# A linear-attention layer with a feed-forward behind it on one core: w and u spread by products on two row halves, both chunks of a pair interleaved, six more transfers that transpose, and another order of all steps

## The chip, the cores and the metric

The kernel runs on one core of a Trainium2 chip. The metric is the device time of one execution in microseconds (us), the median of several runs; lower is better. The engines are TensorE (PE, matrix products and transposes; PEld is its weight load), VectorE (DVE), ScalarE (ACT), GpSimd (POOL) and SyncE (SP, which here only issues DMA transfers). Each engine works through its own list in order and waits by semaphores for the others.

## What is computed

Four batches of eight heads, 768 time steps, head size 48. First a recurrence per head, then a feed-forward over all 3072 tokens (384 features, 2048 hidden).

```python
for t in range(S):                                     # S = 768
    cur = einsum('bhd,bhe->bhde', u[None] * kt, vt)
    y[:, :, t] = einsum('bhd,bhde->bhe', rt, state + cur)
    state = w[None, :, :, None] * state + einsum('bhd,bhe->bhde', kt, vt)
x = y.transpose(0, 2, 1, 3).reshape(B * S, H * D)      # 3072 x 384
h = maximum(x @ w_in, 0.0)                             # 384 x 2048
out = h * h @ w_out                                    # 2048 x 384
```

All inputs and the output are float32 in memory; products run in bfloat16.

## The kernel before

**Units.** The time steps are cut into chunks of 128. A unit is one chunk of one batch, all eight heads: 24 units, listed in UNITS (line 17). Within a chunk the recurrence becomes products: with t the place in the chunk, r is scaled by w to the power t - 128 and k by w to the power 127 - t (factors Wt and Wk), so that the part within the chunk is a masked 128x128 product of r and k per head, times v, and the part of earlier chunks is r times a state S0W. The first four units (PAIRED) are two pairs, two chunks of one batch, loaded with rows of 384 bytes, of which partition p holds time steps 2p and 2p+1; there half of the partitions (64) belong to one chunk and half to the other.

**Steps of one unit** (methods of class Do, one name each): ld (line 319) loads r, k, v of one unit on SP's queue, lp (323) those of a pair. rh (339) and kh (336) scale r and k into a bfloat16 tile rk. P0 (342) is r times k, P1 (345) that times u, du (349) its sum per head, dv (352) v times du: the term of u. vb (357) is v in bfloat16. T (394) transposes rk by eight products with the identity and Tc (400) copies the result to rkT; XB (403) does the same as one DMA that transposes (crossbar transfer), on SP's queue. A (406) is the product of k and r per head, Bm (418) masks it out of PSUM. Y (421) sums the masked product times v, and for a batch's later chunks r times the state. xs (470) adds dv and writes bfloat16. X (486) transposes xs by three products and xTc (491) copies it to xT; xX (495) is one DMA that transposes instead. U (457) is k times v, and S0 (477), ts (480) and S (483) make the next state from it. For the pairs, TK and TR (360, 366) transpose k and r, KC and RC (369, 372) copy, Ap (375) and Bp (391) are A and Bm, and dv enters Y as a product with the identity (lines 427 to 432) instead of in xs.

**Feed-forward.** Units are gathered in groups of one or two (GROUPS). F1 (498) gives one bank of 512 hidden values by 12 products with 128 columns (group of one) or 6 with 256 (group of two), re (512) is the relu out of PSUM, sq (519) the square, F2 (526) four products with 384 columns that sum a quarter of the hidden values into the unit's output bank, os (574) copies it and out (577) stores it. The last unit's F2 is cut into column halves (Fh, COLS), with oh and outh. V and W (330, 333) load the two weight matrices on POOL's queue in four pieces each.

**Start.** w (256) loads the 384 values of w into one row, lw (265) takes their logarithm, bw (268) spreads the row to 128 partitions by a product with a row of ones in float32, and Wk and Wt (292, 296) are exponentials of that with a factor per partition. bc (300), WLcol (308) and WLm (311) make w to the power 128 in the shape of the state. u, bu and ub do the same for u. Z (563) are products without use that keep PE working. tab loads ACT's tables.

**Order.** ORDER (line 25) is a list written out by hand: each entry is step, engine (P, D, A, G for POOL, S) and buffer numbers. The loop at line 595 issues it as it stands, so each engine's list is the part of ORDER with its letter, and a step that waits holds back all that stand behind it on its engine, SP's transfers too.

```python
    for step in ORDER.split():
        what, how = step.split(":")
        name, *at = what.split(".")
        eng, *given = how.split("/")
```

## Time and profile before

| | |
|---|---|
| median of 3 runs | 170.84 us (170.64 to 170.85) |
| profiled execution | 171.19 us |
| its span, first to last instruction | 169.5 us |
| busy, of the span | PE 97%, DVE 81%, ACT 60%, POOL 59% |
| DMA queue of SP (q1) | 66.4% of 16 engines' span |
| weights' queue (q0) | 11.5% |
| granted TensorE clock | 1.0 |

Rows of the timeline read: start in us, duration in us, engine, line, operation, output<-inputs, shapes (partitions x elements), xcount, and in brackets the idle time before and what ended it. Rows by form end with busy us, mean ns of one, and the idle time of the engine before them. The digits under the page's slices are tenths of 40 equal parts of the span. A chain row is start, duration, engine and what it worked on. Times of matrix products in timeline rows overlap; the chain gives their spacing.

### The profile page before, as it was taken

Reading aid. Unit: us, or ns where it says so; the run is one execution under the profiler, and the core shown is the slowest. Engines: PE = TensorE matmul, PEld = TensorE weight load, DVE = VectorE, ACT = ScalarE, POOL = GpSimd, SP = SyncE. Lnnn points to the kernel's source line nnn. Section 1 sums busy time; section 2 is a strip of 40 time slices with the busy share of each in tenths; the row PEclk is TensorE's granted clock in tenths of the full one; section 3 lists DMA queues with packets and bytes.
Section 4 is the critical chain, followed back from the end, with each engine's and each line's share of the span. In section 5 each row is a group of like instructions: output and inputs, shape, how many; then the busy total and the mean of one; then the engine's idle time right before and its main releaser. Section 6 shows DMA issues by size and latency. Waiting matters only on the chain.

```text
span 169.5 us, 4602 instructions
## 1 busy us (share of the span) xinstructions
PE 164.2 (97%) x1828; PEld 125.4 (74%) x1828; DVE 137.1 (81%) x255; ACT 101.9 (60%) x190; POOL 99.9 (59%) x122
## 2 busy tenths in 40 slices
PE   4999999999999999999999999999999999999993
PEld 1686989767866786888766888766888676898762
DVE  5669989997899999979999999998779975955300
ACT  4684686870685779249892359952099393254731
POOL 6799681277199608996699979399627550200000
PEclk9999999999999999999999999999999999999999
DMA  5999999991899798999997999965959672230032
GB/s 136 323 237 193 215 215 208 201 200 39 165 200 211 138 191 173 209 201 134 209 203 151 212 228 220 177 136 141 184 98 202 170 88 70 90 99 0 6 139 93
DMA packets 96137, 27.56 MB, mean 163 GB/s; under 512 B 90642, under 2 KB 96020, under 8 KB 96116
## 3 DMA queue, kind: packets, MB, share of 16 engines
q1 hardware_dynamic: 92416, 22.55, 66.4%
q0 software_dynamic: 2816, 3.54, 11.5%
q10 hardware_dynamic: 884, 1.18, 2.2%
q8 instruction: 14, 0.23, 0.6%
q14 instruction: 7, 0.06, 0.1%
HBM read 20.45 MB, written 4.72 MB: 149 GB/s over the span
## 4 chain that ended last, share of the span: by engine, by line
PE 95%; ACT 1%; DVE 1%; issue 1%; ACTq 0%
PE bank L505 37%; PE bank L533 36%; PE bank L411 3%; PE bank L463 2%; PE bank L452 2%; PE bank L364 2%; PE bank L489 2%; PE bank L450 2%; PE bank L547 2%; PE bank L440 1%; PE bank L269 1%; DVE Bm L392 1%; PE bank L303 1%; PE bank L272 1%; PE bank L398 1%; PE bank L428 1%
## 5 line engine op out<-in xcount | busy, mean ns | idle before, releaser
L505 PE MATMUL bank<-xT,W 128*128 128x256 bf16 (+1 forms) x672 | 70.0, 257 | 0.0
L533 PE MATMUL bank<-W,hq 128*128 128x384 bf16 x368 | 68.9, 326 | 0.0
L505 PEld LDWEIGHTS <-W 128*128 128x128 bf16 x672 | 56.9, 98 | 7.7
L515 ACT ACTIVATE hr<-bank 128x512 bf16<-128x512 f32 x67 | 38.7, 594 | 36.4 <-PE bank L505 27.8
L533 PEld LDWEIGHTS <-hq 128*128 128x128 bf16 x368 | 33.8, 98 | 18.2
L522 ACT ACTIVATE hq<-hr 128x512 bf16<-128x512 bf16 x70 | 41.0, 626 | 3.4 <-DVE hr L517 2.8
L419 DVE TENSOR_TENSOR Bm<-bank,maskJT 128x512 bf16<-128x512 f32 x40 | 25.7, 682 | 2.7 <-PE bank L411 2.7
L355 POOL TENSOR_TENSOR dv<-ldv,du 128x384 f32<-128x384 f32 (+1 forms) x18 | 15.9, 891 | 16.2 <-DVE du L350 11.3
L517 DVE TENSOR_SCALAR hr<-bank 128x512 bf16<-128x512 f32 x29 | 19.7, 686 | 6.6 <-PE bank L505 4.5
L347 POOL TENSOR_TENSOR P<-P,ub 128x384 f32<-128x384 f32 x15 | 16.0, 1070 | 13.1 <-DVE P L343 12.7
L340 POOL TENSOR_TENSOR rk<-ldr,Wt 128x384 bf16<-128x384 f32 x15 | 16.4, 1101 | 0.0
L343 POOL TENSOR_TENSOR P<-ldr,ldk 128x384 f32<-128x384 f32 x13 | 13.3, 1023 | 1.5 <-DMA ldk<-in_k_dram 1.2
L524 DVE TENSOR_TENSOR hq<-hr 128x512 bf16<-128x512 bf16 x26 | 12.4, 490 | 2.0 <-ACT hr L515 1.8
L484 POOL TENSOR_TENSOR S0W<-ts,WLm 128x384 bf16<-128x384 f32 x10 | 10.9, 1091 | 4.4 <-DVE ts L481 3.6
L475 DVE TENSOR_TENSOR xs<-bank,dv 128x384 bf16<-128x384 f32 x20 | 11.1, 553 | 3.0 <-PE bank L452 1.1
L337 POOL TENSOR_TENSOR rk<-ldk,Wk 128x384 bf16<-128x384 f32 x12 | 12.3, 1032 | 1.4 <-DMA ldk<-in_k_dram 1.4
L350 DVE TENSOR_REDUCE du<-P 128x8 f32<-128x384 f32 x24 | 12.9, 542 | 0.0
L253 DVE COPY os<-bank 128x384 f32<-128x384 f32 x11 | 6.1, 551 | 6.9 <-PE bank L533 6.9
L481 DVE TENSOR_TENSOR ts<-bank,S0W 128x384 f32<-128x384 f32 x16 | 8.7, 550 | 1.2 <-POOL S0W L484 0.8
L452 PE MATMUL bank<-vb,Bm 128*128 128x48 bf16 x160 | 9.5, 183 | 0.0
L251 ACT COPY os<-bank 128x384 f32<-128x384 f32 (+2 forms) x14 | 6.3, 458 | 4.5 <-PE bank L533 2.5
L452 PEld LDWEIGHTS <-Bm 128*128 128x128 bf16 x160 | 8.2, 96 | 1.0
(79 smaller groups left out, 177.8 us busy)
## 6 DMA issues: line engine op xcount, KB each, us to landing
ldr<-in_r_dram SPq DMA_DIRECT2D x20, 192.0 KB, 4.0
ldk<-in_k_dram SPq DMA_DIRECT2D x20, 192.0 KB, 4.2
ldv<-in_v_dram SPq DMA_DIRECT2D x20, 192.0 KB, 3.6
out_dram<-os SPq DMA_DIRECT2D x12, 192.0 KB, 2.1
W<-in_moe_w_in_dram POOLq DMA_DIRECT2D x4, 384.0 KB, 8.6
W<-in_moe_w_out_dram POOLq DMA_DIRECT2D x4, 384.0 KB, 6.4
out_dram<-os ACTq DMA_DIRECT2D x5, 192.0 KB, 3.5
ldr<-in_r_dram SPq DMA_DIRECT2D x2, 384.0 KB, 4.1
```

Of the source, the lines that this page charges most:

```text
L340: e.tensor_mul(rk[slot[f"rk{i}"]][:, 0, :, 0:D], loaded("r", i), Do.factor("t", i % 2 if i < PAIRED else 2))
L343: e.tensor_mul(P0b[slot[f"P{i}"]], loaded("r", i), loaded("k", i))
L347: e.tensor_mul(t, t, bank("bu")[:, 0 : H * D].rearrange("p (h d) -> p h d", h=H) if i in EARLY_U else ub)
L350: e.tensor_reduce(dub[slot[f"dv{i}"]], P0b[slot[f"P{i}"]], axis=mybir.AxisListType.X, op=ALU.add)
L355: e.tensor_mul(dv_of(i) if i < PAIRED else dvb[slot[f"dv{i}"]], loaded("v", i), t)
L419: e.tensor_mul(Bmb[slot[f"Bm{i}{h}"]], heads(bank(f"bA{i}{h}"), 128), mask_b)
L452: e.matmul(y[:, hc, D * h : D * (h + 1)], m[h][:, hc, :], vb[:, 2 * hc + h, :], start=(c == 0), stop=True, skip_group_check=True,)
L505: e.matmul(hp[:, fi, :], W1[f // 4][:, c, 256 * (f // 2 % 2) : 256 * (f // 2 % 2 + 1)].rearrange("p (m j) -> p j m", j=2)[:, f % 2, :], xt ...
L515: e.activation(hr, hp, AF.Relu)
L517: e.tensor_scalar_max(hr, hp, 0.0)
L522: e.activation(hq, hr, AF.Square)
L533: e.matmul(bank(f"bO{i}")[:, 0:d_model], hqb[slot[f"hq{g},{f // m}"]][:, at : at + L], W2[q][:, f % 4, :], start=(seen[i] == 1 and f % 4 = ...
```

## The change

- **w and u.** Each is loaded as two rows of 192, on partition 0 and partition 64. bw and bu are two products each, one on each half of PE's rows, into two banks. The product now spreads the raw w, and the logarithm (lw) is taken afterwards, on 128 partitions, half by half; the exponentials read it from SBUF (LW) instead of from PSUM.
- **Pairs.** U of both chunks becomes UP, Y becomes YD (terms of dv and of the masked product, both chunks in turn, which use different row halves and different banks) and YI (the state's term, for the second chunk alone).
- **Transfers that transpose.** XB takes unit 9 as well (T.9 and Tc.9 go), xX the units 10 and 12 to 15 as well (X and xTc of these go).
- **Order.** All of ORDER is another one. Steps of one kind that move between engines, before and after: dv on DVE 6 and 12 of 24, kh 12 and 16, rh 9 and 12, P0 11 and 8, P1 9 and 8, vb 2 and 4; re on DVE 29 and 23 of 96, sq 26 and 34; os on DVE 11 and 7 of 23; outputs issued by ACT 6 and 12 of 23, by SP 15 and 11, by POOL 2 and none. T.5 stands on PE ahead of the first F1, where it stood behind fifteen feed-forward products. The first weights are issued on POOL behind WLm, P0.0 and P0.1. The last steps on PE are Fh with 288 columns, where they had 96. Memsets of the spare columns of rk and of WLm stand in the list, part of them behind rh.2.

```diff
-EARLY_U = ()
 ...
 ORDER = """
+mP.0:G nj:D w:A tab:A bw:P/0/1 u:A Z.4:P/2 lw.0:A Z.4:P/3 lp.r.1:S/1 lw.1:A Wt.0:A/4 lp.r.0:S/0 lp.k.0:S/0 rh.2:D/2
+Wk.0:A/5 lp.k.1:S/1 ld.k.5:S/4 Wk.1:A/6 mR:D mW:D mP.1:G mJ:G Wt.1:A/7 bc:P/0 WLcol:A WLm:G rh.0:D/0 P0.0:G/0 rh.1:D/1
+lp.v.0:S/0 kh.1:D/1 Wt.2:A bu:P/2/1 ub.0:A kh.0:D/0 rh.3:D/3 ub.1:A P1.0:D P0.3:D/1 du.0:D/0 P0.1:G/2 kh.3:D/3
+TR.0:P/3 RC.0:A/0 V.1:G TK.0:P/0 KC.0:A/1 TR.1:P/4 Ap.0.0:P/2/1 RC.1:A/2 P1.1:G kh.2:D/2 TK.1:P/7 V.0:G du.1:D/1
+Ap.0.1:P/3/0 Bp.0.0.0:D/0 vb.0:A/0 vb.1:A/1 KC.1:A/3 Bp.0.0.1:D/1 Bp.0.1.0:D/2 dv.1:G Bp.0.1.1:D/3 UP.0:P/6/5
+Ap.1.0:P/4/2 S0.0:D Ap.1.1:P/1/7 dv.0:G YD.0:P/3/0 V.2:G YI.1:P Wk.2:A P0.2:G/3 lp.v.1:S/1 vb.3:A/2 vb.2:A/3 xs.0:A/0
+Bp.1.0.1:D/4 Bp.1.0.0:D/5 kh.5:D/4 UP.1:P/6/2 X.0:P/3 xs.1:A/1 xTc.0:A/0 ld.r.5:S/4 rh.5:G/4 P1.3:D X.1:P/4 xTc.1:A/1
+T.5:P/0 Tc.5:A/4 F1.0.1:P/3 S0.2:D P1.2:G du.3:D/2 F1.1.1:P/4 F1.0.0:P/6 re.1.1:A/0 du.2:D/3 F1.1.0:P/0 Bp.1.1.0:D/6
+dv.3:G Bp.1.1.1:D/7 dv.2:G re.0.1:A/1 sq.0.1:D/0 re.1.0:A/2 YD.1:P/1/4 xs.2:A/2 A.5:P/7/3 ts.3:D/0 YI.3:P xs.3:A/3
+P0.5:D/4 F1.1.2:P/0 ld.r.4:S/5 V.3:G X.2:P/2 ts.1:D/1 xTc.2:A/0 ld.k.4:S/5 ld.k.8:S/6 X.3:P/1 sq.1.0:A/1 re.0.0:A/3
 ...
+X.6:P/7 F2.0.3:P/2 ld.v.9:S/0 os.0:A/3 XB.9:S/3 ld.r.11:S/3 rh.11:D/3 XB.8:S/0 vb.9:G/0 ld.k.11:S/3 xTc.6:D/2
+ld.r.14:S/7 Y.11:P/6 F2.6.3:P/0 F2.6.0:P/0 xs.10:D/0 vb.13:A/4 P1.11:G du.11:D/3 XB.12:S/1 dv.11:D xs.11:D/2 xX.10:S/1
 ...
+F2.21.1:P/1 sq.13.3:D/15 Fh.23.2.1:P/3 F2.18.2:P/7 os.21:A/1 out.21:S F2.22.2:P/6 Fh.23.3.1:P/3 F2.20.1:P/0
+F2.20.0:P/0 out.12:A out.19:A F2.22.0:P/6 oh.23.1:A/0 outh.23.1:A out.10:S os.20:D/2 out.20:A os.22:D/5 out.22:A
+Fh.23.1.0:P/5 Fh.23.3.0:P/5 Fh.23.2.0:P/5 Fh.23.0.0:P/5 oh.23.0:A/3 os.18:D/4 out.18:S outh.23.0:S
 """
-    Y=["bY{0}"], xs=["xs{0}"], U=["bU{0}"], ts=["ts{0}"], X=["bX{0}"], xTc=["xT"], xX=["xT"],
+    bw=["bW0", "bW1"], bu=["bu0", "bu1"], Y=["bY{0}"], xs=["xs{0}"], U=["bU{0}"], YD=["bY{x}", "bY{y}"], UP=["bU{x}", "bU{y}"], ts=["ts{0}"], X=["bX{0}"], xTc=["xT"], xX=["xT"],
-    bw=["bW"], Wk=["WkP{0}"], Wt=["WtP{0}"], bu=["bu"], bc=["bc"], Fh=["bO{0}{2}"], oh=["os{0}{1}"],
+    Wk=["WkP{0}"], Wt=["WtP{0}"], bc=["bc"], Fh=["bO{0}{2}"], oh=["os{0}{1}"],
 ...
-    wrow = const.tile([1, H * D], FP32, name="wrow")
-    lrow = const.tile([1, H, 64], FP32, name="lrow")
-    urow = const.tile([1, H * D], FP32, name="urow")
-    ones = const.tile([1, 128], FP32, name="ones")
+    wsrc = const.tile([128, H * D // 2], FP32, name="wsrc")
+    usrc = const.tile([128, H * D // 2], FP32, name="usrc")
+    LW = const.tile([128, H, DP], FP32, name="LW")
+    ones = const.tile([128, 128], FP32, name="ones")
     wcol = const.tile([128, HP], FP32, name="wcol")
     Wk = const.tile([128, H, D], FP32, name="Wk")
     Wt = const.tile([128, H, D], FP32, name="Wt")
     WLm = const.tile([128, HP, 2 * D], FP32, name="WLm")
 
-    nc.vector.memset(lrow[:, :, D:64], 0.0)
+    nc.vector.memset(LW[0:1, :, D:DP], 0.0)
     nc.vector.memset(ones, 1.0)
+    for t in rk[:PAIRED]:
+        nc.vector.memset(t[:, :, :, D:DP], 0.0)
 
     tcol_i = const.tile([128, 3], mybir.dt.int32, name="tcol_i")
     for c in range(2):
 ...
     nc.vector.tensor_copy(tcol, tcol_i)
     njcol = const.tile([128, 3], FP32, name="njcol")
-    nc.vector.tensor_scalar(njcol, tcol, -1.0, -1.0, op0=ALU.mult, op1=ALU.add)
     identity = const.tile([128, 128], BF16, name="identity")
     make_identity(nc, identity)
 ...
     mask_p = [per_pair(m) for m in maskP]
-    for t in rk:
-        nc.vector.memset(t[:, :, :, D:DP], 0.0)
-    nc.vector.memset(WLm, 0.0)
 
     E = {"A": nc.scalar, "D": nc.vector, "G": nc.gpsimd, "P": nc.tensor, "S": nc.sync}
 ...
+        def halves(e, t, row):
+            e.dma_start(
+                out=t.rearrange("(a q) n -> a q n", a=2)[:, 0, :],
+                in_=row.rearrange("h d -> (h d)").rearrange("(a n) -> a n", a=2),
+            )
+
         def w(e):
-            e.dma_start(out=wrow, in_=w.rearrange("h d -> (h d)").rearrange("(a n) -> a n", a=1))
+            Do.halves(e, wsrc, w)
 
         def u(e):
-            e.dma_start(out=urow, in_=u.rearrange("h d -> (h d)").rearrange("(a n) -> a n", a=1))
+            Do.halves(e, usrc, u)
+
+        def spread(e, t, to):
+            for h in range(2):
+                at = slice(64 * h, 64 * h + 1)
+                e.matmul(
+                    bank(f"{to}{h}")[:, 0 : H * D // 2], ones[at], t[at], start=True, stop=True, skip_group_check=True,
+                )
+
+        def bw(e):
+            Do.spread(e, wsrc, "bW")
+
+        def bu(e):
+            Do.spread(e, usrc, "bu")
+
+        def spread_half(to, h):
+            return bank(f"{to}{h}")[:, 0 : H * D // 2].rearrange("p (h d) -> p h d", d=D)
+
+        def ub(e, h):
+            copy(e, ub[:, HP * h : HP * (h + 1), :], Do.spread_half("bu", h))
 
         def tab(e):
             e.preload_act_table_set("natural_log_exp_and_others")
 
-        def lw(e):
-            e.activation(lrow[:, :, 0:D], wrow.rearrange("a (h d) -> a h d", h=H), AF.Ln)
-
-        def bw(e):
-            e.matmul(bank("bW")[:, 0 : H * D], ones, lrow[:, :, 0:D], start=True, stop=True)
-
-        def bu(e):
-            e.matmul(bank("bu")[:, 0 : H * D], ones, urow, start=True, stop=True)
-
-        def ub(e):
-            copy(e, ub.rearrange("p a b -> p (a b)"), bank("bu")[:, 0 : H * D])
+        def lw(e, h):
+            e.activation(LW[:, HP * h : HP * (h + 1), 0:D], Do.spread_half("bW", h), AF.Ln)
+
+        def nj(e):
+            e.tensor_scalar(njcol, tcol, -1.0, -1.0, op0=ALU.mult, op1=ALU.add)
+
+        def mR(e):
+            for t in rk[PAIRED:]:
+                e.memset(t[:, :, :, D:DP], 0.0)
+
+        def mW(e):
+            e.memset(WLm, 0.0)
 
 ...
+        def spreading(e, o, scale):
+            e.activation(o, LW[:, :, 0:D], AF.Exp, scale=scale)
+
         def Wk(e, n):
-            o = Do.factor("k", n).rearrange("p a b -> p (a b)")
-            e.activation(o, bank("bW")[:, 0 : H * D], AF.Exp, scale=njcol[:, n : n + 1])
+            Do.spreading(e, Do.factor("k", n), njcol[:, n : n + 1])
 
         def Wt(e, n):
-            o = Do.factor("t", n).rearrange("p a b -> p (a b)")
-            e.activation(o, bank("bW")[:, 0 : H * D], AF.Exp, scale=tcol[:, n : n + 1])
+            Do.spreading(e, Do.factor("t", n), tcol[:, n : n + 1])
 
         def bc(e):
 
             for hc in range(HP):
                 e.matmul(
-                    bank("bc")[:, hc : hc + 1], pair(lrow.rearrange("p (o a) b -> p o a b", o=1), 0, hc), ones[:, 0:1],
+                    bank("bc")[:, hc : hc + 1], pair(LW[0:1].rearrange("p (o a) b -> p o a b", o=1), 0, hc), ones[0:1, 0:1],
                     start=True, stop=True, skip_group_check=True,
                 )
 
 ...
-            e.tensor_mul(t, t, bank("bu")[:, 0 : H * D].rearrange("p (h d) -> p h d", h=H) if i in EARLY_U else ub)
+            e.tensor_mul(t, t, ub)
 ...
+        def half(x):
+            return slice(64 * x, 64 * x + 64)
+
+        def YD(e, q):
+            y = [heads(bank(f"bY{2 * q + x}"), 2 * D) for x in range(2)]
+            for a in range(2):
+                for x in range(2):
+                    e.matmul(
+                        y[x][Do.half(a)], identity[Do.half(x), Do.half(x)],
+                        dv_of(2 * q + a)[Do.half(x)].rearrange("p (a e) d -> p a (e d)", e=2),
+                        start=True, stop=False, skip_group_check=True,
+                    )
+            for hc in range(HP):
+                for h in range(2):
+                    for a in range(2):
+                        for x in range(2):
+                            e.matmul(
+                                y[x][:, hc, D * h : D * (h + 1)],
+                                Bmb[slot[f"Bm{q}{a}{h}"]][Do.half(x), hc, :],
+                                vbb[slot[f"vb{2 * q + a}"]][Do.half(x), 2 * hc + h, :],
+                                start=False, stop=True, skip_group_check=True,
+                            )
+
+        def YI(e, i):
+            y = heads(bank(f"bY{i}"), 2 * D)
+            rT = rkTb[slot[f"rT{i // 2}"]].rearrange("p x y -> p (x y)").rearrange("p (h c t) -> p h c t", h=HP, c=2)
+            for hc in range(HP):
+                e.matmul(
+                    y[:, hc, :], rT[:, hc, i % 2, :], S0W[UNITS[i][0]][:, hc, :],
+                    start=False, stop=True, skip_group_check=True,
+                )
+
         def Y(e, i):
             b, c = UNITS[i]
             y = heads(bank(f"bY{i}"), 2 * D)
-            if i < PAIRED:
-                q, s = i // 2, i % 2
-                rows = slice(64 * s, 64 * s + 64)
-                for a in range(2):
-                    e.matmul(
-                        y[64 * a : 64 * a + 64], identity[rows, rows],
-                        dv_of(2 * q + a)[rows].rearrange("p (a e) d -> p a (e d)", e=2),
-                        start=True, stop=False, skip_group_check=True,
-                    )
-                rT = rkTb[slot[f"rT{q}"]].rearrange("p x y -> p (x y)").rearrange("p (h c t) -> p h c t", h=HP, c=2)
-                for hc in range(HP):
-                    if c > 0:
-                        e.matmul(y[:, hc, :], rT[:, hc, s, :], S0W[b][:, hc, :], start=False, stop=False, skip_group_check=True)
-                for hc in range(HP):
-                    for h in range(2):
-                        for a in range(2):
-                            e.matmul(
-                                y[:, hc, D * h : D * (h + 1)],
-                                Bmb[slot[f"Bm{q}{a}{h}"]][rows, hc, :],
-                                vbb[slot[f"vb{2 * q + a}"]][rows, 2 * hc + h, :],
-                                start=False, stop=True, skip_group_check=True,
-                            )
-                return
             t, m, vb = rkTb[slot[f"rkT{i}"]], [Bmb[slot[f"Bm{i}{h}"]] for h in range(2)], vbb[slot[f"vb{i}"]]
             for hc in range(HP):
                 if c > 0:
                         start=(c == 0), stop=True, skip_group_check=True,
                     )
 
+        def UP(e, q):
+            o = [heads(bank(f"bU{2 * q + x}"), 2 * D) for x in range(2)]
+            for hc in range(HP):
+                for a in range(2):
+                    for x in range(2):
+                        e.matmul(
+                            o[x][:, hc, :],
+                            pair(rk[slot[f"rk{2 * q + a}"]], 1, hc)[Do.half(x)],
+                            vbb[slot[f"vb{2 * q + a}"]][Do.half(x), 2 * hc : 2 * hc + 2, :].rearrange("p a b -> p (a b)"),
+                            start=(a == 0), stop=(a == 1), skip_group_check=True,
+                        )
+
         def U(e, i):
             o = heads(bank(f"bU{i}"), 2 * D)
-            rows = slice(64 * (i % 2), 64 * (i % 2) + 64) if i < PAIRED else slice(0, 128)
-            parts = [i // 2 * 2, i // 2 * 2 + 1] if i < PAIRED else [i]
-            for hc in range(HP):
-                for n in parts:
-                    e.matmul(
-                        o[:, hc, :],
-                        pair(rk[slot[f"rk{n}"]], 1, hc)[rows],
-                        vbb[slot[f"vb{n}"]][rows, 2 * hc : 2 * hc + 2, :].rearrange("p a b -> p (a b)"),
-                        start=(n == parts[0]), stop=(n == parts[-1]), skip_group_check=True,
-                    )
+            for hc in range(HP):
+                e.matmul(
+                    o[:, hc, :], pair(rk[slot[f"rk{i}"]], 1, hc),
+                    vbb[slot[f"vb{i}"]][:, 2 * hc : 2 * hc + 2, :].rearrange("p a b -> p (a b)"),
+                    start=True, stop=True, skip_group_check=True,
+                )
 
         def xs(e, i):
             o, y = xsb[slot[f"xs{i}"]].rearrange("p (a b) -> p a b", a=HP), heads(bank(f"bY{i}"), 2 * D)
```

163 lines of the change are left out of this document (74 added, 89 removed).

## The prediction

> **What bounds the kernel now.** First the page: the busy shares, the slices and the chain that ended last.
>
> ```profile
> span 169.5 us, 4602 instructions
> PE 164.2 (97%) x1828; PEld 125.4 (74%) x1828; DVE 137.1 (81%) x255; ACT 101.9 (60%) x190; POOL 99.9 (59%) x122
> PE   4999999999999999999999999999999999999993
> ...
> DMA  5999999991899798999997999965959672230032
> ...
> PE 95%; ACT 1%; DVE 1%; issue 1%; ACTq 0%
> ```
>
> TensorE (PE) is busy in every slice but the first and last, and 95% of the chain is PE. So a microsecond of PE work that goes is a microsecond gained, unless PE then waits; and whatever moves the first F1, the first feed-forward product, moves the end. The DMA engines stand at 9 through most of the first two thirds, and VectorE (DVE) is busy for 81%: they are next in line. Then the timeline of the start.
>
> ```profile
> 1.97 1.03 PE L565 MATMUL bank<-identity 128*128 128x512 bf16 x2 [1.97 <-DVE njcol L214]
> ...
> 2.67 0.52 ACT L266 ACTIVATE lrow<-wrow 1x384 f32<-1x384 f32 x1
> ...
> 3.24 1.64 PE L269 MATMUL bank<-lrow,ones 1*128 1x384 f32 x2 [0.24 <-ACT lrow L266]
> ...
> 4.92 0.56 ACT L298 ACTIVATE bank<-bank,tcol 128x384 f32<-128x384 f32 x1 [1.73 <-PE bank L269]
> ...
> 12.85 2.49 DVE L392 TENSOR_TENSOR Bm<-bank,maskP 128x512 bf16<-128x512 f32 x4 [1.30 <-PE bank L384]
> ...
> 18.13 1.06 PE L505 MATMUL bank<-xT,W 128*128 128x128 bf16 x16
> ```
>
> The start is a chain of latencies: w lands, logarithm, product, exponentials, factors, transposes, masked products, and only at 18.13 the first F1. From there PE does not rest. The chain in order of time prices its pieces.
>
> ```profile
> 22.31 0.28 PE bank L428 x2
> 22.59 0.28 PE bank L436 x4
> ...
> 23.65 0.50 PE bank L440 x16
> ...
> 25.93 0.46 PE bank L398 x8
> ...
> 51.91 0.55 PE bank L398 x8
> ...
> 65.22 0.55 PE bank L411 x16
> ...
> 74.09 0.17 PE bank L489 x3
> ...
> 166.63 0.24 ACT os L251
> ```
>
> **The change part by part.**
>
> *Start.* Before, ACT took the logarithm of one row of 384 (0.52), and the product on 384 columns follows (1.64). Now the product spreads the raw w, each half on its own rows, so it needs no ACT: it can begin when PE first ran, about 2.0 (1.97 above; w had landed before ACT's 2.67). With 192 columns a half it costs 0.8 if the halves run side by side and 1.64 if not; I take 1.2, ending at 3.2. Two logarithms of 128x192 follow. The trace has none; the copy of 96 columns at the very end (0.24, row 166.63 below) and the 0.52 bound one, so I take 0.35 each: 3.9. The first exponential then starts 1.0 before its 4.92.
>
> What becomes of that 1.0? Four exponentials and WLcol end at 3.9 + 4 x 0.56 + 0.2 = 6.3. POOL's queue then sets the pace:
>
> ```profile
> 10.55 1.00 DVE L350 TENSOR_REDUCE du<-P 128x8 f32<-128x384 f32 x2
> ...
> 12.75 0.74 POOL L314 COPY WLm<-wcol 48x192 f32<-48x192 f32 x2
> 13.56 1.01 POOL L343 TENSOR_TENSOR P<-ldr,ldk 128x384 f32<-128x384 f32 x1
> ```
>
> WLm to 7.0, P0.0 and P0.1 at 1.0 each to 9.0, the issue of the first weights (2.50/3, 0.8 to 0.95; row 6.55 further on) to 10.0, P1.1 like P0 to 11.0, and du.1 on DVE, which stands ahead of the masked products there and waits for P1.1, 0.5 more: the first masked product starts at 11.6 instead of 12.85. DVE's factors, ready by then, don't set it. Then, as before, the four products (2.49), UP, S0, YD, xs, X. Y needs dv.0 and dv.1 from POOL by then; they end at about 13.4, covered. Ahead of the first F1 stands one step that was behind it, T.5 (0.46, the first L398 row). First F1 at 17.5: **-0.6** (bounds -1.2, all of the 1.0 kept and more; +0.9, nothing kept and T.5 added on top with a wait).
>
> *PE work behind the first F1.* T.5 has gone ahead of it (-0.46). T.9 becomes a transfer (-0.55). Five X become transfers (5 x 0.17 = -0.85). The second pair's Y ran from 22.31 to 23.65 + 0.50 = 24.15, 1.84: twice two products with the identity (0.28), twice 16 with the values (0.50), once four with the state (0.28). Interleaved, neighbours use different row halves. The A row is the nearest: 16 products of 128 columns that alternate two row groups took 0.55, or 0.034 each, so alternating overlaps them there (one transpose of 128 columns costs 0.17/3 = 0.057). Side by side in full it would be 0.28 + 0.28 + 0.50 = 1.06, with no overlap 1.84; I take 1.4 (-0.45). UP stands ahead of the first F1 in both and is in the start's sum. Together **-2.3** (bounds -1.85 and -2.65).
>
> *Early stage, 18 to 34.* Twenty F1 stand ahead of the first F2 (15 before), and DVE has a longer list first: from the first masked product to xTc.4, on which the F1 of group 3 hang, 37 steps. Twelve masked products at 0.62 (2.49/4) are 7.5, the other 25 lie between 0.5 and 0.8 by the rows here and below, at 0.55 13.8: 21.3 in all, from 11.6 to 32.9. PE wants xTc.4 after 16 F1 at 0.65 (the F2 row below; F1 has as many columns), Y, A, T.4 and X (3.5): 17.5 + 13.9 = 31.4. So PE waits 1.5 if every step takes its mean, and not at all if DVE's steps follow one another as closely as the two du (1.00 for both, 0.50 each): **+0.6** (bounds 0 and 2.0). The weights of these F1 are issued two or more F1 ahead of what needs them; I count them at nothing, and a wait there belongs to the early-load rival.
>
> *Middle.* The steps that change engine, by form:
>
> ```profile
> L517 DVE TENSOR_SCALAR hr<-bank 128x512 bf16<-128x512 f32 x29 | 19.7, 686 | 6.6 <-PE bank L505 4.5 <-ACT hr L515 1.4
> L524 DVE TENSOR_TENSOR hq<-hr 128x512 bf16<-128x512 bf16 x26 | 12.4, 490 | 2.0 <-ACT hr L515 1.8
> L343 DVE TENSOR_TENSOR P<-ldr,ldk 128x384 f32<-128x384 f32 x11 | 7.6, 701 | 0.0
> L337 DVE TENSOR_TENSOR rk<-ldk,Wk 128x384 bf16<-128x384 f32 x8 | 6.1, 768 | 0.0
> L347 DVE TENSOR_TENSOR P<-P,ub 128x384 f32<-128x384 f32 x9 | 6.1, 681 | 0.0
> L253 DVE COPY os<-bank 128x384 f32<-128x384 f32 x11 | 6.1, 551 | 6.9 <-PE bank L533 6.9
> L355 DVE TENSOR_TENSOR dv<-ldv,du 128x384 f32<-128x384 f32 x6 | 4.7, 785 | 0.0
> L340 DVE TENSOR_TENSOR rk<-ldr,Wt 128x384 bf16<-128x384 f32 x5 | 4.0, 800 | 0.0
> ```
>
> DVE gains 6 dv (4.7), 4 kh (3.1), 3 rh (2.4) and 8 squares (3.9); it loses 3 P0 (2.1), 1 P1 (0.7), 6 relus (4.1) and 4 os (2.2): +5.0. Of other copies 2 vb come and 4 xTc, one Tc and one xs go, four fewer in all, worth 0 to -2.2 by the os row; I take -1.1, so net +3.9. POOL loses 6 dv, 4 kh and 3 rh and gains 3 P0 and 1 P1. Where is that felt?
>
> ```profile
> 60.00:110.00 50.00, 50.00 (x546) 39.05 (x544) 47.77 (x84) 34.57 (x66) 38.77 (x40) 1.00 1.01 192
> ```
>
> In this row (span, then PE, PEld, DVE, ACT, POOL, clock, DMA share, GB/s) DVE has 2.2 of 50 idle, PE none, and the DMA engines are full. The extra 3.9 spreads over all stages, and DVE works ahead of PE by buffered results, so most of it is hidden: **+0.8** (bounds 0 and 3.9). The moved steps have two operands in SBUF:
>
> ```profile
> L337 POOL TENSOR_TENSOR rk<-ldk,Wk x12: 987/997/1316, 40.2 to 114.5; 128x384 bf16<-128x384 f32 x12
> L337 DVE TENSOR_TENSOR rk<-ldk,Wk x8: 546/636/1181, 21.9 to 132.7; 128x384 bf16<-128x384 f32 x8
> L337 DVE TENSOR_TENSOR rk<-ldk,bank x4: 541/550/555, 6.0 to 9.6; 128x384 bf16<-128x384 f32 x4
> ```
>
> With a PSUM operand the same step is steady at 0.55; with two in SBUF it takes up to 1.18. [...]
>
> The six transfers cost PE nothing while other products stand between. An xX lands 2.3 after its issue where X took 0.17 and a copy:
>
> ```profile
> xT<-xs SPq DMA_TRANSPOSE x8, 2.3
> ```
>
> ```profile
> 58.52 0.65 PE bank L533 x4
> ```
>
> Between Y.10 and the first F1 of its group stand nine F1 and F2 on PE; seven of them F2 at 0.65 by the last row, so 4.6 and more cover the 2.3. Without that cover each of the six would cost up to 1.8, which is part of the first rival.
>
> *End.* The last products are now of 288 columns instead of 96, so the last copy is longer than 0.24, and its output larger; **+0.2** (bounds 0 and 0.5). Two outputs fewer on POOL and some on ACT's queue hide beside the other work.
>
> **Sum:** -0.6 - 2.3 + 0.6 + 0.8 + 0.2 = -1.3 on the profiled execution, 171.19 (span 169.5 and 1.7 around it), that is 169.9. The median of the runs, 170.84, is 0.35 lower: **169.5**.
>
> **The rivals.**
>
> *The late transfers fall behind (slower).* 60 to 110 has no spare DMA time (1.01), and 97% of it is one queue:
>
> ```profile
> q1 hardware_dynamic: 40672, 8.94, 97.0%
> ```
>
> One XB of 256 KiB and five xX of 96 KiB add 0.75 MB, at the row's 192 GB/s 3.9 us. It decides once the loads land after POOL and DVE want them. Against it: PE never waited for a load, and the share falls after 110. If it all reaches PE, in place of the 0.8: -2.1 + 3.9 = +1.8, **172.6**. [...]
>
> *The early load is late (slower).* T.5 now stands ahead of the first F1 and needs rh.5, so ld.r.5. The weights' and its own issue before, and issue to landing of the single loads issued in the first 12 us:
>
> ```profile
> 6.55 2.50 POOL L331 DMA_DIRECT2D W<-in_moe_w_in_dram  x3
> 6.68 1.15 SPq L321 DMA_DIRECT2D ldr<-in_r_dram  x1
> ```
>
> ```profile
> ldr<-in_r_dram SPq DMA_DIRECT2D x2, 192.0 KB, 12.9
> ```
>
> ld.r.5 was the 6.68 issue; now it is one load later, near 7.9. The weights, issued at 6.55 before, now stand on POOL behind WLm, P0.0 and P0.1, so about 2.5 later; that is what should save it. If it still takes 9 to 10, rh.5 (1.1) and T.5 put the first F1 near 19.3, 1.8 later than forecast: +0.5, **171.3**; with 12.9 worse.
>
> *DVE becomes the bound.* In place of 0.8, 3.9 less the idle 2.2 = 1.7: -0.4, **170.4**; for it 47.77 of 50, against it POOL's shorter list beside it.
>
> *The row halves take turns.* The product keeps 1.64, Y keeps 1.84, 0.9 is lost: **170.4**; the A row speaks against it.
>
> **How the numbers follow.** Forecast 0.45, late transfers 0.17, early load 0.13, DVE 0.15, halves 0.10. A measurement of this kernel tells about 0.2% (0.35 us) from no change. Faster: 0.43 of the forecast's 0.45, 0.08 of the halves, 0.07 of DVE and 0.03 of the two others, 0.61. Slower: 0.15 from the late transfers, 0.09 from the early load, 0.05 from the rest, 0.29. Same: 0.10. All good bounds together give -1.2 - 2.65 = -3.85, 167.0; they seldom meet, so the range begins at 167.5, and it ends just above the late transfers, 172.8.
>
> **What would show it.** Right: first F1 before 18.0 and T.5 ahead of it; the second pair's Y under 1.5; no transpose on PE after some 90; DVE near 141 busy with PE still at 9 throughout. Wrong: PE idle with a DVE, DMA or transfer releaser between 60 and 130; T.5 waiting for rh.5; a first F1 later than 18.6.

## The result

After takes 188.07 us in the median of 4 runs (185.64 to 188.7), before 170.74 beside it. Two of after's four executions were disturbed, so all times, ratios and differences from here on are medians of undisturbed executions, against undisturbed ones of before on the same chip: 186.64 for after, a ratio of 1.093 (95% interval 1.083 to 1.103). The forecast was 169.5 with a range up to 172.8: it has the sign wrong, and some 16 us are to be explained.

The page of after (profiled execution 187.65), the lines shown of before, and with them DVE's slices and the clock:

```profile
span 185.9 us, 4554 instructions
...
PE 163.1 (88%) x1803; PEld 122.7 (66%) x1803; DVE 146.8 (79%) x258; ACT 103.3 (56%) x196; POOL 89.2 (48%) x107
...
PE   1959888979999985995999999898995999999993
...
DVE  2799999989596799899929899999989776561211
...
PEclk9996999999999999998799999999999999999999
DMA  5999988999949999953994979999896602110154
...
PE 50%; DVE 27%; issue 7%; DMA 7%; POOL 4%; ACT 2%; SPq 1%; DVEq 0%; POOLq 0%; ACTq 0%
```

PE has less work than before, as the change meant it to, but only by 1.1 us (163.1 for 164.2). And it idles: 185.9 - 163.1 = 22.8 us against 169.5 - 164.2 = 5.3. The chain is only half PE now, and 27% of it is DVE, which had 1%. DVE is busy for 9.7 us more. By stages (stretch, its length, busy PE, PEld, DVE, ACT, POOL, clock, DMA share, GB/s):

```profile
0.00:18.00 18.00, 11.61 (x152) 8.34 (x154) 13.15 (x30) 11.15 (x20) 11.45 (x28) 0.93 1.00 224
18.00:34.00 16.00, 13.45 (x247) 11.41 (x242) 15.84 (x24) 11.03 (x20) 12.68 (x15) 0.98 0.96 166
34.00:60.00 26.00, 24.12 (x232) 17.29 (x230) 22.45 (x41) 13.73 (x27) 8.69 (x10) 1.00 1.07 138
60.00:110.00 50.00, 44.46 (x477) 33.28 (x476) 42.77 (x70) 31.44 (x63) 30.99 (x30) 0.97 0.88 171
110.00:150.00 40.00, 36.66 (x393) 27.86 (x391) 37.99 (x65) 19.70 (x37) 25.35 (x26) 1.00 0.88 172
```

PE's idle time is 6.4, 2.6, 1.9, 5.5 and 3.3 in these five stages, where before had 2.4 in the first and none in the other four: no single stall, but a loss in each. In the second and fifth DVE is at 99% and 95%. What ended PE's longest waits (total, times, longest):

```profile
PE bank L529 <- DVE xs L515: 4.8, 3, 2.1
PE bank L267 <- DMA wsrc<-in_w_dram: 3.7, 1, 3.7
PE bank L387 <- DVE rk L360: 2.4, 1, 2.4
PE bank L545 <- DVE xT L249: 2.2, 3, 1.6
PE bank L545 <- DVE dv L378: 2.1, 1, 2.1
```

Apart from the load of w at the start all of these end with DVE. And DVE's steps became longer, not only more. The groups of products with two operands in SBUF (count | busy, mean ns), beside the prediction's rows of before (567 here for 490, 901 for 768, 892 for 785, 936 for 681):

```profile
L564 DVE TENSOR_TENSOR hq<-hr 128x512 bf16<-128x512 bf16 x34 | 18.8, 567 | 7.6 <-ACT hr L555 7.4
...
L360 DVE TENSOR_TENSOR rk<-ldk,Wk 128x384 bf16<-128x384 f32 x12 | 10.8, 901 | 0.0
L378 DVE TENSOR_TENSOR dv<-ldv,du 128x384 f32<-128x384 f32 x12 | 10.7, 892 | 0.2
...
L370 DVE TENSOR_TENSOR P<-P,ub 128x384 f32<-128x384 f32 x8 | 7.5, 936 | 0.1
```

One of them in the timeline, DVE above and POOL below:

```profile
23.73 1.99 DVE L564 TENSOR_TENSOR hq<-hr 128x512 bf16<-128x512 bf16 x1
```

```profile
23.59 0.80 POOL L354 DMA_DIRECT2D W<-in_moe_w_in_dram  x1
24.41 1.01 POOL L363 TENSOR_TENSOR rk<-ldr,Wt 128x384 bf16<-128x384 f32 x1
```

The square begins at 23.73, and it is done at 25.72, 0.30 after POOL's rh has ended at 25.42. POOL's rh took its usual 1.01 (0.99 is the shortest of its kind in after, 1.01 the median); the square took 1.99, where 0.41 is the shortest of its kind and 0.42 the median. The time was lost on DVE. Ahead of rh POOL was issuing a weight's transfer for 0.80; how much of the square's 1.99 belongs to that is not shown.

### The profile page after: what moved, and what is told of

It is laid out like the page before. It is cut to its first block, busy times and chain, and to the rows that moved or that the text cites. A ratio compares the mean times of both kernels' runs of the same rounds, so it can differ in the third digit from the quotient of the medians.

```text
span 185.9 us, 4554 instructions
## 1 busy us (share of the span) xinstructions
PE 163.1 (88%) x1803; PEld 122.7 (66%) x1803; DVE 146.8 (79%) x258; ACT 103.3 (56%) x196; POOL 89.2 (48%) x107
## 4 chain that ended last, share of the span: by engine, by line
PE 50%; DVE 27%; issue 7%; DMA 7%; POOL 4%; ACT 2%; SPq 1%; DVEq 0%; POOLq 0%; ACTq 0%
PE bank L545 22%; PE bank L573 21%; DMA ldr<-in_r_dram 5%; DVE Bm L442 4%; DVE hq L564 3%; DVE dv L378 3%; DVE hr L557 3%; DVE rk L363 2%; DVE xs L515 2%; DVE P L366 2%; PE bank L434 2%; DVE du L373 2%; DMA wsrc<-in_w_dram 2%; PE bank L587 1%; POOL P L366 1%
## 5 line engine op out<-in xcount | busy, mean ns | idle before, releaser
L555 ACT ACTIVATE hr<-bank 128x512 bf16<-128x512 f32 x73 | 41.9, 597 | 34.1 <-PE bank L545 31.2
L562 ACT ACTIVATE hq<-hr 128x512 bf16<-128x512 bf16 x62 | 37.6, 630 | 6.1 <-DVE hr L557 5.7
L564 DVE TENSOR_TENSOR hq<-hr 128x512 bf16<-128x512 bf16 x34 | 18.8, 567 | 7.6 <-ACT hr L555 7.4
L366 POOL TENSOR_TENSOR P<-ldr,ldk 128x384 f32<-128x384 f32 x16 | 18.0, 1129 | 5.6 <-DMA ldk<-in_k_dram 5.5
L557 DVE TENSOR_SCALAR hr<-bank 128x512 bf16<-128x512 f32 x23 | 15.5, 682 | 2.7 <-PE bank L545 1.8
L524 POOL TENSOR_TENSOR S0W<-ts,WLm 128x384 bf16<-128x384 f32 x10 | 10.9, 1094 | 12.7 <-PE bank L484 4.6
L363 POOL TENSOR_TENSOR rk<-ldr,Wt 128x384 bf16<-128x384 f32 x12 | 13.2, 1100 | 6.1 <-DMA ldr<-in_r_dram 6.1
L378 POOL TENSOR_TENSOR dv<-ldv,du 128x384 f32<-128x384 f32 (+1 forms) x12 | 10.1, 848 | 7.9 <-DVE du L373 7.9
L247 ACT CAST vb<-ldv 128x384 bf16<-128x384 f32 x14 | 6.9, 513 | 8.0 <-DMA ldv<-in_v_dram 8.0
L378 DVE TENSOR_TENSOR dv<-ldv,du 128x384 f32<-128x384 f32 x12 | 10.7, 892 | 0.2
L360 DVE TENSOR_TENSOR rk<-ldk,Wk 128x384 bf16<-128x384 f32 x12 | 10.8, 901 | 0.0
```

Source lines behind the costliest of these rows:

```text
L363: e.tensor_mul(rk[slot[f"rk{i}"]][:, 0, :, 0:D], loaded("r", i), Do.factor("t", i % 2 if i < PAIRED else 2))
L366: e.tensor_mul(P0b[slot[f"P{i}"]], loaded("r", i), loaded("k", i))
L378: e.tensor_mul(dv_of(i) if i < PAIRED else dvb[slot[f"dv{i}"]], loaded("v", i), t)
L555: e.activation(hr, hp, AF.Relu)
L557: e.tensor_scalar_max(hr, hp, 0.0)
L562: e.activation(hq, hr, AF.Square)
```

## The experiments

Three theories. **Lockout:** in the new order DVE's two-operand products and POOL's products meet more often, and DVE's are longer where they meet (the 1.99 above); DVE becomes the bound and PE waits for it. **SyncE's queue:** transfers that transpose wait for their data and hold the loads behind them. **Start:** w's two-row load is late and everything after it. Later a fourth: the **parts** themselves (pairs, transfers) cost, whatever the order. One table of all runs; the time is the median, idle is the span less PE's busy time, in the profiled execution.

| run | us | ratio to before | PE idle | DVE busy |
|---|---|---|---|---|
| before | 170.7 to 171.0 | | 5.3 | 137.1 |
| after | 186.64 | 1.093 (1.083 to 1.103) | 22.8 | 146.8 |
| e1 after, old start | 185.41 | 1.086 (1.083 to 1.089) | 19.9 | 146.4 |
| e2 after, fills on POOL | 178.72 | 1.046 (1.041 to 1.051) | 14.4 | 126.1 |
| e3 after, free transfers | 188.50 | 1.103 (1.096 to 1.111) | 23.9 | 145.5 |
| e4 before, fills on POOL | 172.90 | 1.012 (1.009 to 1.014) | 7.2 | 126.9 |
| e5 after, fills and free transfers | 186.57 | 1.089 (1.081 to 1.097) | 21.5 | 126.5 |
| e6 before's order, after's engines | 191.07 | 1.121 (1.110 to 1.131) | 19.6 | 144.7 |
| e7 after's order, before's engines | 200.52 | 1.174 (1.159 to 1.188) | 33.1 | 141.3 |
| f1 before, pairs | 169.76 | 0.993 (0.991 to 0.995) | 6.0 | 136.4 |
| f2 before, pairs, transfers | 183.63 | 1.071 (1.067 to 1.076) | 17.0 | 133.8 |
| f3 before, all three parts | 182.81 | 1.067 (1.063 to 1.071) | 16.3 | 133.8 |
| g1 before, pairs, rows | 172.09 | 1.007 (1.003 to 1.011) | 8.2 | 135.9 |
| g2 after, no added transfers | 188.51 | 1.105 (1.099 to 1.110) | 22.2 | 143.8 |
| g3 as g2, old start | 187.88 | 1.099 (1.094 to 1.104) | 21.9 | 144.0 |
| g4 as g3, fills on POOL | 180.25 | 1.057 (1.050 to 1.063) | 13.5 | 125.8 |
| h1 after, old start, fills, free transfers | 175.50 | 1.027 (1.020 to 1.034) | 12.2 | 126.8 |
| h2 before, pairs, XB.9 | 170.16 | 0.995 (0.994 to 0.997) | 6.3 | 136.1 |
| h3 after, half the squares off DVE | 183.71 | 1.073 (1.066 to 1.080) | 19.7 | 138.6 |
| k1 after, copies on POOL | 188.93 | 1.107, no interval | 23.0 | 131.7 |

### Lockout: e2, its control e4, k1 and h3

```diff
-    e.tensor_mul(o, a, b)                       # on POOL: kh, rh, P0, P1, dv, S
+    e.memset(o, 0.01)                           # e2, e4; in k1: e.tensor_copy(o, a)
+    e.memset(o, 0.01)
+    e.tensor_mul(o[:, :, 0:1], a[:, :, 0:1], b[:, :, 0:1])
```

> After, with every product on GpSimd (kh, rh, P0, P1, dv, S) replaced by two fills of its whole output and the product on one column of each head: GpSimd stays about as busy and hardly reads SBUF; that part of the output is not computed. VectorE and GpSimd against each other: VectorE's busy time falls from 146.8 to 123 to 128, no kh, rh, dv or sq step on VectorE over 1.2 us, PE's idle time from 22.8 to under 10, time 172 to 177. SyncE's queue held, or late head: VectorE's steps may shrink, but PE still waits, time 184 to 188.

> Before, with the same replacement on GpSimd, as the control of that edit (that part of the output is not computed). VectorE and GpSimd against each other: VectorE's busy time falls by about 10 us, but PE idles only 5.3 us in before, so the time falls by 0 to 3 us, to 168 to 171. If instead the edit frees something that has nothing to do with these two engines, before gains as much as after does in the run beside it, 8 us or more.

e2's products of DVE (count: shortest/median/longest in ns):

```profile
L365 DVE TENSOR_TENSOR rk<-ldk,Wk x12: 548/550/569, 17.6 to 118.1; 128x384 bf16<-128x384 f32 x12
L365 DVE TENSOR_TENSOR dv<-ldv,du x12: 546/553/559, 27.8 to 148.6; 128x384 f32<-128x384 f32 x12
```

The same in after:

```profile
L360 DVE TENSOR_TENSOR rk<-ldk,Wk x12: 546/762/1837, 18.7 to 128.3; 128x384 bf16<-128x384 f32 x12
...
L378 DVE TENSOR_TENSOR dv<-ldv,du x12: 541/762/1927, 30.7 to 158.0; 128x384 f32<-128x384 f32 x12
```

POOL is as busy as before the edit (90.4 for 89.2 us), yet DVE's products are at 0.55 throughout (one P1 of 0.87 is the longest of all): the stretching is gone when POOL fills. And DVE's busy time without it is 126.1 in after's list and 126.9 in before's: **the two lists hold the same work.** What DVE spends above that is stretching, 146.8 - 126.1 = 20.7 us in after and 137.1 - 126.9 = 10.2 in before. DVE has 88 such products in after and 71 in before, so 0.235 us each for 0.144; with before's 0.144 the 88 would make 12.7. By this estimate some 2.5 of the 10.5 more come from the number and 8 from how they meet.

The time agrees: after falls by 7.9 us, before gains nothing and loses 2, outside the 168 to 171 expected (probably since the three instructions delay POOL, which stands on 12% of e4's chain). So the edit as such makes a kernel no faster; it helps where PE waits for DVE. At 178.7 e2 is still above the 172 to 177 expected, and PE idles 14.4 where under 10 was expected. The longest waits of PE in e2 say what is left:

```profile
PE bank L553 <- DMA xT<-xs: 5.0, 3, 2.8
PE bank L267 <- DMA wsrc<-in_w_dram: 3.8, 1, 3.8
```

The waits for DVE that headed after's list are gone (0.4 for xs and 0.3 for rk are left). In their place stand three waits for transfers that transpose, which after did not show, probably because they landed there while PE waited for DVE; two of them, 3.0 us, are for transfers that the change added. So more than the lockout is lost in after.

> As e2, but each of the two fills is a copy of the product's first operand over the same output, which reads SBUF (that part of the output is not computed). If GpSimd's reading keeps VectorE's two-operand products waiting: VectorE's kh and dv are at 0.7 us or more in the mean again where e2 had 0.55, VectorE is busy for 135 us or more, and the time is 183 to 190. If e2's gain came from the shorter instructions or from something else in the edit: 0.55, 126 and 177 to 180 as in e2.

k1 answered neither way: kh and dv are at 0.594 and 0.600, DVE is busy for 131.7, so 5.6 of the 20.7 us of stretching came back with the reading. But POOL's copies, which read one operand, take 0.53 to 0.63 in the mean, where its products, which read two, take 1.00 to 1.03 in the median in after (dv 0.83), and POOL's three instructions now add up to more (112.3 us busy for 89.2), which alone may account for its 188.9. It shows DVE's products of 128x384 with two SBUF operands longer beside POOL's copies (0.59 to 0.75 in the mean, by step) than beside its fills (0.55 to 0.60 in e2); how much hangs on the length of POOL's instruction it leaves open.

> After with every second of VectorE's 34 squares on ScalarE (17 steps of 0.567, 9.6 us off VectorE, 10.7 onto ScalarE, which is 56% busy). If VectorE is the bound where PE waits: 3 to 8 us faster, 180 to 185. If its stretching is a symptom and the waits come from loads and transfers: within 2 us of 188. If ScalarE's own order makes the squares late: slower.

```diff
-sq.0.1:D/0        # and every second of the 34 squares on D
+sq.0.1:A/0
```

In a kernel that computes everything, 17 steps less on DVE (busy 138.6, 8.2 less) give some 3 us, and the intervals of the two ratios do not meet: at the low end of what DVE as the bound should give, and against the view that DVE's load is only a symptom.

### SyncE's queue: e3, e5, h1

```diff
-    e.dma_start_transpose(out=rkTb[...], in_=rk[...])      # XB; xX alike from xs
+    e.dma_start_transpose(out=rkTb[...], in_=rk_free)      # filled once at the start
```

> After, with every crossbar transfer reading a constant tile that is there from the start, so that none holds SyncE's queue and the loads behind it go out early; the transposed values are not those of the data. SyncE's queue held: ld.r.4 and ld.r.11 land 3 to 5 us earlier, no wait of PE ends with a load, time 172 to 178. VectorE and GpSimd against each other, or late head: time 184 to 188, VectorE's busy time within 2 us of 146.8.

e3 gains nothing (188.5). PE's waits for DVE are as in after, but a stall of 4.7 us has come in with the edit:

```profile
PE bank L534 <- DVE xs L520: 4.8, 3, 2.1
PE bank L578 <- ACT hr L560: 4.7, 1, 4.7
```

ACT stood at an output for 5.7 us there, as it does for longer in e5 below. So e3 leaves open whether loads that come earlier would be of use while PE waits for DVE.

> After, with both earlier edits at once: GpSimd's products replaced by fills and one column of each head, and every crossbar transfer reading a constant tile, so that none holds SyncE's queue (both parts of the output are not computed). If the excess is VectorE against GpSimd first, with SyncE's held queue as the bound right behind it, the time falls from 178.7 (fills alone) to 171 to 174. If the rest of the excess is the late head or the order itself, it stays at 176 to 179.

Missed: 186.6, 8 us slower than e2. The waits of PE and ACT's timeline tell why:

```profile
PE bank L586 <- ACT hr L568: 12.7, 1, 12.7
PE bank L272 <- DMA wsrc<-in_w_dram: 3.9, 1, 3.9
PE bank L464 <- POOL dv L368: 0.6, 1, 0.6
```

```profile
103.20 0.36 ACTq L639 DMA_DIRECT2D out_dram<-os  x1
103.60 0.63 ACT L575 ACTIVATE hq<-hr 128x512 bf16<-128x512 bf16 x1 [13.63 <-DMA ldk<-in_k_dram]
```

Only the start and one stall are left. ACT came to an output at about 90, and the profile puts the end of its wait down to a load of k landing. SP issued such a load at 100.07, the only one between 91 and 105; its queue was issuing for 9 of every 10 us up to 120. Behind the output stood relus and squares, so all stopped. What ties an output to a load of k, with nothing in the data between them, is not shown.

> After with before's start, GpSimd's products replaced by fills, transfers that read constant tiles, and the outputs that ScalarE issued early given to SyncE (those two parts of the output are not computed). If VectorE's stretching and SyncE's held queue, with the start, are the whole loss: no long wait of PE, 172 to 175, within 2 us of before with the same fills (173.0). If the order of the compute keeps a share: 177 or more, with PE's waits scattered over VectorE, ScalarE and GpSimd.

With the early outputs of ACT given to SP (`out.7:A` becomes `out.7:S`, and so on) and the old start, 175.5, ratio 1.027, between the two guesses. PE's longest waits are then 2.2 (a weight piece), 2.0 (the first one, until POOL has made the identity) and 2.0 (a relu on DVE). e2's gain and e1's together would give 177.5, so freeing the queue has given some 2 us at most, too little to be told from two executions (174.49 and 176.52).

### Start: e1, g1

```diff
-bw:P/0/1 u:A Z.4:P/2 lw.0:A Z.4:P/3 lp.r.1:S/1 lw.1:A
+lw:A u:A Z.4:P/2 Z.4:P/3 bw:P/0/1 lp.r.1:S/1
```

> After's order, with before's way of spreading w and u (one row each, one float32 product each, exponentials from the bank). Late head (the two-row load of w holds up everything): first masked product back from 14.67 to about 13, first F1 from 21.07 to about 18.5, and if the head is the whole loss the time is 171 to 173. VectorE and GpSimd against each other: the head gives back at most 2 us, VectorE stays over 145 us busy, and the time is 185 to 188. SyncE's queue held: 185 to 188 too.

> Before's order and engines with the pairs of f1 and with w and u as two rows each, no added transfers. If the two-row loads come late (products at 3.7, masked products 12.25 to 13.3): 0.5 to 1.3 us over f1's 169.8, so 170.3 to 171.1. If the spread is worth what it was meant for: 169.2 to 169.5.

e1 lies 1.2 us under after, which after's own scatter covers; 14.5 over before are left. Its first F1 comes at 20.33, not near 18.5, so w's load is the smaller part of the late head. g1 is at 172.1, 2.3 over f1, more than expected. The start of after (ACT, PE, and the load in the chain):

```profile
0.81 1.10 ACTq L253 DMA_DIRECT2D wsrc<-in_w_dram  x1
1.94 1.28 ACT L284 ACT_TABLE_LOAD   x1 [1.94 <-issue]
...
4.75 0.55 ACT L287 ACTIVATE LW<-bank 128x192 f32<-128x192 f32 x2 [1.53 <-PE bank L267]
5.34 0.58 ACT L315 ACTIVATE bank<-LW,tcol 128x384 f32<-128x384 f32 x1
```

```profile
3.74 1.01 PE L267 MATMUL bank<-wsrc,ones 1*128 1x192 f32 x4 [3.74 <-DMA wsrc<-in_w_dram]
```

```profile
0.81 2.80 DMA wsrc<-in_w_dram
```

The products side by side take 1.01, as hoped. But they start at 3.74: the issue of the two-row load takes 1.10 where one row took 0.53, the load ends at 3.61 where before's row was there by 2.67, and the first exponential comes at 5.34 instead of 4.92.

### Parts and order: f1 to f3, g2 to g4, e6, e7, h2

> Before's order, engines and start, with only U and Y of the first two pairs as after has them (the products of both row halves in turns). If the new products do what they are for: 0.4 to 1.0 us less on PE's path, 169.8 to 170.5. If row halves only take turns: 170.6 to 171.0. If the waits for both chunks' operands cost: up to 171.5. If after's loss lies in these products: 172 or more.

```diff
-U.1:P/5 ... U.0:P/6 ... Y.0:P/1 ... Y.1:P/6
+UP.0:P/6/5 ... YD.0:P/1/6 YI.1:P            # and the second pair alike
```

f1 is the fastest kernel of this study, ratio 0.993 (0.991 to 0.995), some 1.2 us. The second pair's Y in f1:

```profile
21.59 0.36 PE L436 MATMUL bank<-dv,identity 64*64 64x384 bf16 x4
21.88 0.57 PE L445 MATMUL bank<-vb,Bm 64*128 64x48 bf16 x32
22.38 0.34 PE L456 MATMUL bank<-S0W,rkT 128*128 128x96 bf16 x4
22.64 0.83 PE L530 MATMUL bank<-xT,W 128*128 128x128 bf16 x12
```

From 21.59 to the F1 at 22.64 it is 1.05, 0.8 less than before's 1.84: 32 products in the time of 16 (0.50, from 21.88 to 22.38), so here the row halves run side by side in full. The first F1 comes at 17.47 instead of 18.13, 0.7 earlier; UP now stands on PE behind the first Ap, where U.1 stood ahead of it.

> The same, and six more crossbar transfers in before's order in place of T.9 and X.10, X.12 to X.15 with their copies. If PE's work is the bound and the transfers are hidden: 1.4 us less than the run without them, 168.4 to 169.4. If the added transfers hold SyncE's queue and loads come late (about 1.2 to 1.6 us of issue each, and each waits for a product of VectorE): 171 to 176. If after's loss lies in the transfers alone: 178 or more.

```diff
-T.9:P/4 ... Tc.9:A/0 ... X.10:P/3 ... xTc.10:A/1      # X.12 to X.15 alike
+XB.9:S/0 ... xX.10:S/1
```

In before's order the transfers cost some 14 us, and PE waits for them directly (timeline, and the stretches beside it):

```profile
79.34 1.46 PE L529 MATMUL bank<-xT,W 128*128 128x256 bf16 x6 [3.63 <-DMA xT<-xs]
...
80.92 3.91 PE L529 MATMUL bank<-xT,W 128*128 128x256 bf16 x18
```

```profile
70.00:75.00 5.00, 5.00 (x57) 4.34 (x54) 4.15 (x9) 3.33 (x6) 5.00 (x6) 1.00 0.98 205
75.00:80.00 5.00, 1.37 (x11) 0.86 (x9) 5.00 (x8) 2.30 (x5) 3.10 (x3) 0.77 0.95 170
80.00:85.00 5.00, 5.00 (x29) 3.53 (x28) 0.78 (x1) 2.54 (x5) 0.49 (x1) 0.54 1.02 202
```

The transfer behind this wait was issued at 76.46 and landed at 79.29, where X and its copy had stood next to each other on PE and ACT. Three such waits are 11.2 us. In the stretch behind the first (3.63) the granted clock is 0.54, and 18 products take 3.91 us, where 18 took 2.13 at 69.12 and a clock of 1.00. After the second (2.88) it is 1.00, and 18 take 2.14. From 110 to 115, around the third (4.68), it is 0.69.

> Before's order and engines with all three parts: pairs, six transfers, and w and u as two rows each. If the late two-row load is as in after (its products at 3.7 where before had the exponentials at 4.9, masked products about 1 us later): 0.5 to 1.5 us over the run without it. If the spread in two halves is worth what it was meant for: 0.3 to 0.6 below it. If the whole loss of after is in its order and engines, all three runs lie within 3 us of before; if in the parts, this one is at 180 or more.

182.8, 0.8 below f2 and not above it: the waits for transfers are 8.8 us in three here, 2.4 less than in f2, which hides what the start costs. This run says nothing on rows that g1 doesn't say better.

> After with the six added transfers undone (T.9 and X.10, X.12 to X.15 on PE again with copies on ScalarE, each at the place of its transfer). If the transfers are the larger part of the loss, as in before's order: 174 to 179. If VectorE against GpSimd is the bound in front of them: 185 to 188. If they were a gain of 1.4 us of PE's work: 188 to 190.

> The same with before's way of spreading w and u. If the start adds to the rest, as in e1: 2 to 2.5 us below g2. If g2's time is set behind the start by something that the start doesn't move: as g2 within 1 us.

> The same with GpSimd's products replaced by fills and one column of each head (that part of the output is not computed). If stretching, transfers and start are the whole loss: 170 to 173. If the order keeps a share of its own (transfers and loads behind waiting ones, GpSimd's steps due too late): 174 to 178.

The guess that f2 had found the cause fell at once: taken out of after, the transfers give nothing back (188.5, and the 1.9 us more are within the scatter of after), so after's order seems to give them room. g3 is as g2 within 1 us. g4 lies 7.6 below g3, the fills' gain once more, and at 180.3 it keeps 7.4 us over e4 that neither the start nor the added transfers explain.

> Before's order, with each step on the engine that after gives it (166 steps change engine; on VectorE 17 products of two SBUF operands more, of kh, rh, dv, sq, and fewer P0 and P1). If the choice of engines makes the stretching, VectorE's busy time rises from 137 to over 144 and the time to 178 to 188. If the order makes it, 170 to 174, with VectorE at 139 to 142.

> After's order, with each step on the engine that before gives it. If the choice of engines makes the loss, the time falls to 171 to 176. If the order makes it (steps meet that did not meet before, and transfers stand behind waiting ones), it stays at 183 or more; it may be longer, since this order was not made for these engines.

Both edits leave the outputs on the engines that the order had them on. Both kernels are slower than before and after, so they don't split the loss into an order's share and an engines' share: each list holds only with its own engines. One thing can be read: with after's engines before's order has 144.7 us on DVE, 7.6 more, most of after's 9.7, as expected if the choice of engines makes the stretching; its time, 191.1, is above what was expected either way.

> f1 (before's order with the pairs) and one of the six transfers, XB.9 in place of T.9 and its copy. If it has room where it stands: 0.3 to 0.6 us below f1's 169.8 (T.9 is 0.55 of PE's time), 169.1 to 169.5. If it holds loads behind it: 170.5 or more.

h2 is faster than before but not faster than f1: T.9's 0.55 is not regained.

## Why the prediction was wrong

- **Middle, the step that failed.** It put DVE's added steps at their means of before (+3.9) and "most of it is hidden: +0.8". Both halves failed. The means hold before's meetings with POOL, and they are no property of the step: kh and dv take 0.55 beside POOL's fills (e2), 0.77 and 0.79 in before, 0.90 and 0.89 in after. And they weren't hidden: the five stages show PE waiting in each. The prediction's own rows have kh on DVE at anything from 0.55 to 1.18 with two operands in SBUF, but its sum has no term for more of that, and against DVE as the bound it put POOL's shorter list. That list is shorter (107 instructions for 122), but DVE has 17 more of the products that stretch, and they stretch by twice as much in all (20.7 us for 10.2). The fills give back 7.9 us, where the sum had +0.8: the stretching was the missing term.
- **Start, -0.6.** Measured: first F1 at 21.07, 2.9 later than before. Of its steps, the product took 1.01 (1.2 assumed), the logarithms 0.55 together (0.35 each), but the product began at 3.74 and not at 2.0: that w had landed by then was read off a one-row load. POOL ended P1.1 at 12.47 instead of 11.0, since it began WLm late, at 7.78. But what set the masked products' 14.67 was DVE, which the prediction took to be ready (first POOL, then DVE):

```profile
7.78 0.74 POOL L337 COPY WLm<-wcol 48x192 f32<-48x192 f32 x2 [3.42 <-DVE rk L363]
...
11.46 1.01 POOL L370 TENSOR_TENSOR P<-P,ub 128x384 f32<-128x384 f32 x1
```

```profile
9.64 1.34 DVE L370 TENSOR_TENSOR P<-P,ub 128x384 f32<-128x384 f32 x1
10.90 1.99 DVE L366 TENSOR_TENSOR P<-ldr,ldk 128x384 f32<-128x384 f32 x1
...
14.67 1.87 DVE L415 TENSOR_TENSOR Bm<-bank,maskP 128x512 bf16<-128x512 f32 x3
```

  Two products that take 0.55 each in e2's median took 3.2 beside POOL's P0.0, P0.1, a weight's issue and P1.1: lockout again. The first F1 tells what each is worth: 21.07 in after, 20.33 with the old start (e1), 19.82 with the fills (e2), 19.08 with both (h1, where the transfers are free as well), 18.13 in before. So of the 2.9 some 0.7 are the spread, 1.3 the lockout, and 0.9 are left for the list itself. T.5 waited 0.82, for kh.5 on DVE, not for rh.5 as the early-load rival had it.
- **PE work, -2.3.** Right where it could be seen: the second pair's Y 1.05 (1.4 assumed; the good bound 1.06), f1 faster by some 1.2, of which 0.7 come ahead of the first F1. In after the gain is lost in waits, and PE's busy time falls by 1.1 only; the granted clock, 0.93 and 0.97 in the two stages where PE idles longest (6.4 and 5.5) and 1.0 in before's, may have taken part of the rest.
- **Early stage, +0.6.** The mechanism was right: DVE is at 99% and PE idles 2.6 in 18 to 34, 0.82 of it ahead of T.5. The working was not: DVE's list to xTc.4 has 34 steps and not 37, which by the same means ends at 31.2 and gives no wait at all. The size fell short, for 2.1 more follow right behind, where PE waits for a dv that took 1.93; the square of 1.99 stands here too.
- **Transfers.** No cost that could be seen in this order (g2), but with the fills, when PE hardly waits for DVE, two waits for added transfers cost PE 3.0 (e2). The rival of late transfers is not what happened in after, though two loads of r stand on its chain (5.2 and 4.4 us in flight); DVE itself waited 0.9 for one of them, POOL 6.1 for two.
- **"DVE becomes the bound"** was a rival with 0.15 and 170.4. It was the right mechanism; its price was again the mean of before's rows.

**What stays open.** Lockout (7.9, and perhaps 2 more that the fills themselves cost, by e4) and the start (1.2 by e1, 2.3 by g1 against f1) account for most of the 16. In h1 2.6 us over e4 are left, scattered over waits for DVE, POOL, ACT and a weight piece, and in g4, which keeps the queue as it is, 7.4. How these split between the order of the compute and SyncE's queue was not separated: e3 and e5, made for the queue, brought in a stall of their own.

## What to carry to other kernels

In these runs the mean duration of a VectorE product with two SBUF operands went with the schedule, not with the step (kh 0.55 in e2, 0.77 in before, 0.90 in after): price such a product from its shortest (0.55 here) plus the time it may lose beside GpSimd's products, and ask of a new order which of them will stand side by side. Where VectorE stood at 95% in a stage (60 to 110 in before), added work was not hidden by buffers: PE, which never idled there in before, idles 5.5 us in after. And take a change apart: the interleaved pairs alone, in the old order, are 0.7% faster than before, while the whole is 9% slower.
